# Plain float32 matmuls in the first chunk, with the split of its weights moved: one fused attention and MoE kernel

## The chip, the cores and the metric

The kernel runs on one core of a Trainium2 chip. The core has five engines that work side by side from their own queues: TensorE (PE, matmuls; PEld its weight loads), VectorE (DVE), ScalarE (ACT), GpSimd (POOL) and SyncE (SP), which here issues most DMAs. The metric is the device time of one execution in microseconds (us); lower is better.

## The reference, cut to what matters

Three layers follow each other on 4 x 576 = 2304 tokens. First windowed attention with 8 heads of 64; then a dense layer; then a layer with 8 experts, of which each token takes one.

```python
scores = scale * q @ k.T, kept where 0 <= row - col < 64
x = softmax(scores) @ v                       # 2304 x 512
h = x @ w_in                                  # w_in 512 x 2048
g = where(h >= 1, h, where(h <= -1, 0, (h + 1) ** 2 / 4))
x = g @ w_out                                 # w_out 2048 x 512
logits = x @ w_gate + modality_bias[modality_id]
e = argmax(logits);  out = gate_w * relu(x @ w1[e]) @ w2[e]
```

`w_in` and `w_out` come as 64 bit floats. [...]

## The kernel before

**Chunks and steps.** The tokens are cut into 6 chunks of 384 (`CT`). One chunk goes through 16 steps (`NF`), one for each block of 128 hidden units. Step f has `l1(c, f)`: 4 blocks of `w_in` against the chunk's x, result h in PSUM (2 buffers); then `act2` and `gsplit`; and, two steps later (`LAG`), `l2(c, f)`: matmuls of 512 columns that add to three sums `py`. Between the steps the attention of the next chunk's six blocks of 64 tokens is computed (`att_sc`, `att_exp`, `att_norm`, `att_tr`, `att_pv`, `att_x`); chunk 0's own six blocks run ahead of everything. After the chunk, `route` finds the experts. From some 520 us on, the expert layer runs in slots of 256 tokens; the change leaves it alone but for the names of the weight tiles.

**Precision by parts.** TensorE reads each operand as a rounded type, float32r. A float32 operand is kept as a rounded part (`hi`: a ScalarE copy) and the rest (`lo`: a subtraction), and a product is three matmuls: hi hi, hi lo, lo hi. So `l1` is 12 matmuls of 384 columns (L370) and `l2` 9 of 512 (L396). The scores (L292), the transposes (L330) and attention's second product (L345) are matmuls in plain float32.

**Decoding.** Chunk 0 is where the weights are decoded. They come in 16 pairs of 128 x 512 tiles: pair p, from 3 on, is block p - 1 of `w_out` and block p + 1 of `w_in`. The pair's words are loaded by SyncE (L237) to one of two buffers in `dec`. ScalarE takes the absolute value (`dec_abs`, L243). VectorE then runs four instructions for each tile: `dec_clamp` (L250, L252) and `dec_merge` (L258, L262). `dec_split` rounds on ScalarE (L270) and subtracts on GpSimd (L272), into `bigA` for `w_in` and `wB` for `w_out`. GpSimd also has `gsplit`'s subtraction in chunk 0 (L386) and `att_norm`'s multiplication (L323). Three pairs are decoded ahead of chunk 0 (`PRE`); then one in each step.

**Order.** A scheduler sets the order in the engines' queues from its own timeline; each queue then runs in that order. Only SyncE's order is written out by hand.

Of the kernel before, what the change touches and what calls it, by code (L numbers as in the profile page):

```python
# [9 lines left out]
F32 = mybir.dt.float32  # L10
F32R = mybir.dt.float32r
# [6 lines left out]
P = 128  # L18
# [52 lines left out]
def moe_kernel(ctx, tc, qT, kT, v, w_in, w_out, mod, wg, wgT, mbias, w1, w2, cst, tri, empty, out, spec):  # L71
# [11 lines left out]
        shape[axis] = n  # L83
        return a.broadcast_to(shape)

    WIDE = {"bigA", "dec", "prod", "q", "k", "v", "xh", "xl", "y", "s", "ts", "u", "gh", "gl"}
    WIDE |= {f"B{f}" for f in range(NF)}

    def tile_of(shape, name, dt=F32, tag=None, bufs=1):
        pool = sb if (tag or name) in WIDE else sm  # L90
# [3 lines left out]
        return ps.tile(shape, F32, name=name, tag="aux", bufs=3)  # L94

    WB = KD * P
    bigA = tile_of([P, NF * 2 * WB], "bigA", F32R)
    bigB, lent = {}, {}

    def piece(b, n):  # L100
        if not b:
            return bigA[:, n * WB : (n + 1) * WB]
        f, lo = divmod(n, 2)
        if f not in bigB:
            bigB[f] = tile_of([P, 2 * WB], f"wB{f}", F32R, tag=f"B{f}")
        return bigB[f][:, lo * WB : (lo + 1) * WB]

    def lend(f, lo, n=WB):
        if f not in lent:
            lent[f] = tile_of([P, 2 * WB], f"lent{f}", tag=f"B{f}")  # L110
        return lent[f][:, lo * WB : lo * WB + n]

    GB = 2
# [3 lines left out]

    def load_q(i):
        if i < BPC - 2:
            t = lend(2 + i // 2, i % 2)  # L120
        else:
            t = tile_of([P, WB], f"q{i}", tag="q", bufs=2)
        SP.dma_start(t, qT[i])
        qs[i] = t.rearrange("p (k n) -> p k n", k=KD)

    def load_k(g):
        t0 = g * GT
        k0 = max(t0 - BLK, 0)
        if g * GB < BPC:
            k_t = lend(7 + g, 0, KD * (GT + BLK)).rearrange("p (k n) -> p k n", k=KD)  # L130
# [147 lines left out]
    def new_x(c):  # L278
        xs[c] = tuple(tile_of([P, KD, CT], f"x{s}{c}", F32R, tag=f"x{s}", bufs=2) for s in "hl")

    at, xos = {}, {}

    def att_sc(i):
        q_t = qs.pop(i)
        k_t, k0 = ks[i // GB]
        n, w0 = window(i)
        if i < BPC:
            sc = ps.tile([P, KD, P], F32, name=f"sc{i}", tag=f"y{i % TT}", bufs=1)
        else:
# [454 lines left out]
    def half_slot(i, g, x, mid):  # L744
# [50 lines left out]
    for n in range(BPC + 3):  # L795
# [30 lines left out]
    for n in range(len(its) + LAG):  # L826
# [155 lines left out]
```

## Time and profile before

| What | us |
|---|---|
| median of 3 runs (785.8 to 785.94) | 785.9 |
| the profiled execution | 785.36 |
| its span in the trace | 783.7 |
| TensorE busy in the span | 732.9 |
| VectorE, ScalarE, GpSimd busy | 519.8, 418.3, 215.8 |
| chunk 0, first L370 to last L396 on TensorE | 33.2 to 152.0 |
| chunk 1 behind it, to its last L396 | 152.0 to 231.9 |

How to read it: an engine's busy time is a sum over stages that have different limits, so the table by itself does not tell what a change of one stage is worth. The trace is read by stretches instead. A matmul's time in a row overlaps its neighbour's; what it costs in a stream is the distance from one start to the next, which the chain of work shows as the sum for several. The granted clock is a share of TensorE's full 2.4 GHz.

### The profile page before, as it was taken

Reading aid. Unit: us, or ns where it says so; the run is one execution under the profiler, and the core shown is the slowest. Engines: PE = TensorE matmul, PEld = TensorE weight load, DVE = VectorE, ACT = ScalarE, POOL = GpSimd, SP = SyncE. Lnnn points to the kernel's source line nnn. Section 1 sums busy time; section 2 is a strip of 40 time slices with the busy share of each in tenths; the row PEclk is TensorE's granted clock in tenths of the full one; section 3 lists DMA queues with packets and bytes.
Section 4 is the critical chain, followed back from the end, with each engine's and each line's share of the span. In section 5 each row is a group of like instructions: output and inputs, shape, how many; then the busy total and the mean of one; then the engine's idle time right before and its main releaser. Section 6 shows DMA issues by size and latency. Waiting matters only on the chain.

```text
span 783.7 us, 13640 instructions
## 1 busy us (share of the span) xinstructions
PE 732.9 (94%) x4547; PEld 650.7 (83%) x4547; DVE 519.8 (66%) x1449; ACT 418.3 (53%) x973; POOL 215.8 (28%) x266
## 2 busy tenths in 40 slices
PE   7389796999999999999999999989997999999995
PEld 6377575988898889888898889878886989998994
DVE  4999999596349643964396648845765575656560
ACT  5565666645454544555455445534425565555551
POOL 2665667311201120102010232031047144432100
PEclk9689898999999999999999999999998999999998
DMA  9564463521222231222122105235547776766650
GB/s 325 170 217 144 166 217 109 213 70 42 55 59 80 65 62 48 82 69 61 48 82 62 14 1 182 74 55 165 172 95 222 236 229 218 225 220 226 216 189 18
DMA packets 55776, 101.90 MB, mean 130 GB/s; under 512 B 8032, under 2 KB 17376, under 8 KB 55568
## 3 DMA queue, kind: packets, MB, share of 16 engines
q1 hardware_dynamic: 50976, 90.91, 37.6%
q0 software_dynamic: 4576, 9.79, 4.1%
q8 instruction: 38, 0.62, 0.4%
q14 instruction: 42, 0.34, 0.1%
q10 hardware_dynamic: 144, 0.24, 0.1%
HBM read 91.46 MB, written 9.83 MB: 129 GB/s over the span
## 4 chain that ended last, share of the span: by engine, by line
PE 75%; DVE 13%; DMA 6%; issue 4%; ACT 1%; POOL 0%; SPq 0%; POOLq 0%; ACTq 0%; DVEq 0%
PE h L370 22%; PE py L396 22%; PE hp L707 11%; PE yo L730 11%; DMA wr<-in_w 3%; DVE dt L258 3%; PE sc L292 3%; DVE dt L250 3%; DVE dt L262 2%; PE xo L345 2%; DVE dt L252 1%; PE pt L330 1%; PE tp L693 1%; DMA dec<-in_w_in 1%; DVE u L379 1%
## 5 line engine op out<-in xcount | busy, mean ns | idle before, releaser
L370 PE MATMUL h<-xh,bigA 128*128 128x384 f32 x768 | 225.3, 354 | 15.4 <-DVE u L379 13.5
L396 PE MATMUL py<-wB,gh 128*128 128x512 f32 x576 | 181.8, 399 | 0.0
L370 PEld LDWEIGHTS h<-xh,bigA 128*128 128x128 f32 x768 | 144.0, 194 | 21.0 <-DVE u L379 15.5
L370 PE MATMUL h<-xl,bigA 128*128 128x384 f32 x384 | 132.1, 344 | 3.1 <-DVE xl L360 3.1
L396 PEld LDWEIGHTS py<-wB,gh 128*128 128x128 f32 x576 | 108.2, 192 | 17.2
L396 PE MATMUL py<-wB,gl 128*128 128x512 f32 x288 | 113.2, 398 | 0.9 <-POOL gl L386 0.8
L379 DVE SCALAR_TENSOR_TENSOR u<-u,h 128x384 f32<-128x384 f32 x96 | 52.9, 551 | 79.8 <-ACT u L374 78.4
L323 POOL TENSOR_TENSOR s<-s,sm 128x512 f32<-128x512 f32 (+1 forms) x30 | 34.2, 1140 | 220.6 <-DVE sm L322 95.7
L373 ACT ACTIVATE u<-h,half 128x384 f32<-128x384 f32 x96 | 55.3, 576 | 69.5 <-PE h L370 68.7
L453 DVE CUSTOM_DVE_ANT_0 prod<-y,wgb 128x512 f32<-128x512 f32 x120 | 85.4, 712 | 1.2
L385 ACT CAST gh<-u 128x384 fp32r<-128x384 f32 x96 | 49.3, 513 | 64.3 <-PE py L396 33.8
L370 PEld LDWEIGHTS h<-xl,bigA 128*128 128x128 f32 x384 | 74.7, 195 | 5.3 <-DVE xl L360 3.6
L643 ACT CAST bigA<-wr 128x512 fp32r<-128x512 f32 x80 | 48.5, 619 | 46.1 <-DMA wr<-in_w 40.2
L644 DVE TENSOR_TENSOR bigA<-wr,bigA 128x512 fp32r<-128x512 f32 x80 | 53.7, 688 | 27.7 <-ACT bigA L643 22.3
L644 DVE TENSOR_TENSOR wB<-wr,wB 128x512 fp32r<-128x512 f32 x80 | 53.1, 686 | 25.9 <-ACT wB L643 24.5
L396 PEld LDWEIGHTS py<-wB,gl 128*128 128x128 f32 x288 | 54.3, 189 | 14.4 <-POOL gl L386 3.0
L386 DVE TENSOR_TENSOR gl<-u,gh 128x384 fp32r<-128x384 f32 x80 | 45.0, 563 | 30.6 <-ACT gh L385 29.2
L643 ACT CAST wB<-wr 128x512 fp32r<-128x512 f32 x80 | 47.7, 619 | 27.2 <-DMA wr<-in_w 26.9
L738 POOL DMA_INDIRECT out<-ob,oi x19 | 20.0, 1051 | 153.0 <-ACT ob L737 119.0
L707 PE MATMUL hp<-zh,bigA 128*128 128x256 f32 x320 | 61.5, 288 | 0.0
L312 ACT ACTIVATE s<-s,mx 128x128 f32<-128x128 f32 (+1 forms) x120 | 46.1, 386 | 28.1 <-DVE mx L302 28.1
L730 PE MATMUL yo<-bigA,hm 128*128 128x512 f32 x240 | 57.5, 392 | 0.0
(203 smaller groups left out, 1324.9 us busy)
## 6 DMA issues: line engine op xcount, KB each, us to landing
wr<-in_w SPq DMA_DIRECT2D x160, 256.0 KB, 3.7
q<-in_qT SPq DMA_DIRECT2D x32, 256.0 KB, 3.8
dec<-in_w_in SPq DMA_DIRECT2D x16, 512.0 KB, 5.3
dec<-in_w_out SPq DMA_DIRECT2D x16, 512.0 KB, 3.7
v<-in_v SPq DMA_DIRECT2D x27, 256.0 KB, 2.5
k<-in_kT SPq DMA_DIRECT2D x15, 384.0 KB, 4.3
yd<-y SPq DMA_DIRECT2D x18, 256.0 KB, 2.8
wgb<-in_wgT SPq DMA_DIRECT2D x1, 2048.0 KB
```

The costliest lines, as they stand in the source:

```text
L312: A.activation(s[:, hp, :n], s[:, hp, :n], AF.Exp, bias=mx[:, hp : hp + 1], scale=-1.0, accum_out=sm[:, hp : hp + 1],)
L370: T.matmul(h, wi(f, a)[:, k, :], b[:, k, :], start=n == 0, stop=n == 3 * KD - 1)
L373: A.activation(u, h, AF.Relu, bias=half, scale=0.5)
L379: V.scalar_tensor_tensor(u, u, 1.0, h, op0=ALU.min, op1=ALU.max)
L385: A.copy(gh, u)
L386: (V if c else G).tensor_tensor(gl, u, gh.bitcast(F32), op=ALU.subtract)
L396: T.matmul(ys[c][t], a[:, sl], wo(f, b), start=f == 0 and n == 0, stop=f == NF - 1 and n == 2)
L453: V.tensor_tensor_reduce(prod, yt[t], wgb[0][:, e, :], 1.0, 0.0, ALU.mult, ALU.add, lg[:, t, e : e + 1])
L643: A.copy(wpart(i, p, 0), t)
L644: V.tensor_tensor(wpart(i, p, 1), t, wpart(i, p, 0).bitcast(F32), op=ALU.subtract)
L707: T.matmul(hp[:, u, :], w1s(i, 2 * fp + u, k, a), b[:, k, :], start=n == 0, stop=n == 3 * KD - 1,)
L730: T.matmul(yo, a[:, f, sl], w2s(i, f, b), start=n == 0, stop=n == 3 * NF2 - 1)
```

## The change

In chunk 0 the products are plain float32: `l1` is 4 matmuls of 384 columns and `l2` 3 of 512, on the decoded weights whole (`whole`), on an x that is not split, and on a g that is not split. The last decoding instruction writes the whole weight to a tile `raw` rather than in place. The two rounded parts are made by a new function `split`, ScalarE's copy and VectorE's subtraction; the code calls it for 6 weights in each of the last three steps of chunk 0 and for 2 in each step of chunk 1. `bigA` and the `wB` tiles become 32 tiles with the tags T0 to T31, which hold whole words first and parts later. GpSimd has none of the split; its normalisation of chunk 0's attention blocks goes to VectorE, that of chunk 1's blocks to ScalarE as four copies with a scale.

```diff
-    bigA = tile_of([P, NF * 2 * WB], "bigA", F32R)
+    def raw_home(p, u):
+        j = 2 * p + u
+        if j == 2 * NF - 1:
+            return dts[p][u]
+        if j // 2 not in raws:
+            raws[j // 2] = tile_of([P, 2 * WB], f"raw{j // 2}", I32, tag=f"T{j // 2}")
+        return raws[j // 2][:, j % 2 * WB : (j % 2 + 1) * WB]
...
             for u in range(2):
+                w = raw_home(p, u)
                 V.scalar_tensor_tensor(
-                    t[u], words(p, u)[0], 29, t[u], op0=ALU.logical_shift_right, op1=ALU.bitwise_or
+                    w, words(p, u)[0], 29, t[u], op0=ALU.logical_shift_right, op1=ALU.bitwise_or
                 )
-
-    def dec_split(p):
-        if p < NPR:
-            t = dts.pop(p)
-            for u, (kind, f) in enumerate(pairs[p]):
-                A.copy(piece(kind, 2 * f), t[u].bitcast(F32))
-            for u, (kind, f) in enumerate(pairs[p]):
-                G.tensor_tensor(
-                    piece(kind, 2 * f + 1), t[u].bitcast(F32), piece(kind, 2 * f).bitcast(F32), op=ALU.subtract
-                )
+                whole[pairs[p][u]] = w.bitcast(F32)
+    whole = {}
+    splits = [kf for p in pairs for kf in p]
+
+    def split(n):
+        for kind, f in splits[:n]:
+            k = len(parts)
+            tag = f"T{2 * NF - 2 + k if k < 2 else NF - 2 + k if k < NF else k - NF}"
+            t = tile_of([P, 2 * WB], f"w{kind}_{f}", F32R, tag=tag)
+            parts[kind, f] = (t, tag)
+            w = whole.pop((kind, f))
+            hi, lo = t[:, :WB], t[:, WB:]
+            A.copy(hi, w)
+            V.tensor_tensor(lo, w, hi.bitcast(F32), op=ALU.subtract)
+        del splits[:n]
...
-        G.tensor_tensor(s, s, bc(sm, 2, window(i)[0]), op=ALU.mult)
+        if BPC <= i < 2 * BPC:
+            w = window(i)[0]
+            for hp in range(KD):
+                A.activation(s[:, hp, :w], s[:, hp, :w], AF.Copy, scale=sm[:, hp : hp + 1])
+            return
+        (V if i < BPC else G).tensor_tensor(s, s, bc(sm, 2, window(i)[0]), op=ALU.mult)
...
-        for k in range(KD):
+        for k in range(KD if c == 0 else 0):
+            T.matmul(h, whole[0, f][:, k * P : (k + 1) * P], xs[c][:, k, :], start=k == 0, stop=k == KD - 1)
+        xh, xl = xs[c] if c else (None, None)
+        for k in range(KD if c else 0):
...
+        if c == 0:
+            g = gs.pop((c, f))
+            for t in range(TT):
+                T.matmul(
+                    ys[c][t], g[:, t * P : (t + 1) * P], whole[1, f], start=f == 0, stop=f == NF - 1
+                )
+            return
...
-            dec_split(f + PRE - 1)
             dec_abs(f + PRE)
+        if c == 0 and f >= NF - PRE:
+            split(6)
+        if c == 1:
+            split(2)
```

The order that results is told here at three places. On GpSimd, early in chunk 0, before (`bigA` and `wB` are weight parts, `gl` is the rest of g):

```order
35 L272 TENSOR_TENSOR bigA<-dt_0_391,bigA 128x512
36 L272 TENSOR_TENSOR wB_440<-dt_1_392,wB_440 128x512
37 L272 TENSOR_TENSOR wB_506<-dt_0_444,wB_506 128x512
38 L272 TENSOR_TENSOR bigA<-dt_1_445,bigA 128x512
39 L386 TENSOR_TENSOR gl_0_500<-u_0_485,gh_0_499 128x384
40 L272 TENSOR_TENSOR wB_568<-dt_0_511,wB_568 128x512
```

and now; the last two rows are for blocks 12 and 13, which are chunk 2's attention:

```order
22 L179 TENSOR_TENSOR btok<-modf,mb 128x144
23 L180 TENSOR_TENSOR btmp<-modn,mb 128x144
24 L181 TENSOR_TENSOR btok<-btok,btmp 128x144
25 L346 TENSOR_TENSOR s_1158<-s_1158,sm_1168 128x512
26 L346 TENSOR_TENSOR s_1249<-s_1249,sm_1261 128x512
```

GpSimd's queue holds nothing between the token biases and chunk 2's attention. On VectorE, around step 3 of chunk 0, before (`dt` are weights being decoded, `u` is the activation):

```order
137 L250 TENSOR_SCALAR dt_0_635<-dt_0_635 128x512
138 L258 SCALAR_TENSOR_TENSOR dt_1_574<-dec,dt_1_574 128x512
139 L252 TENSOR_SCALAR dt_0_635<-dt_0_635 128x512
140 L250 TENSOR_SCALAR dt_1_636<-dt_1_636 128x512
141 L262 SCALAR_TENSOR_TENSOR dt_1_574<-dec,dt_1_574 128x512
142 L379 SCALAR_TENSOR_TENSOR u_3_652<-u_3_652,h_3_639 128x384
143 L258 SCALAR_TENSOR_TENSOR dt_0_635<-dec,dt_0_635 128x512
```

and now (L258, L260, L266, L271 are the four decoding lines, L288 the split, L410 the activation):

```order
142 L410 SCALAR_TENSOR_TENSOR g_3_597<-u_3_580,h_3_575 128x384
143 L266 SCALAR_TENSOR_TENSOR dt_0_527<-dec,dt_0_527 128x512
144 L260 TENSOR_SCALAR dt_1_528<-dt_1_528 128x512
145 L288 TENSOR_TENSOR w_3_1082<-raw_498,w_3_1082 128x512
146 L288 TENSOR_TENSOR w_5_1085<-raw_498,w_5_1085 128x512
147 L271 SCALAR_TENSOR_TENSOR raw_545<-dec,dt_0_527 128x512
148 L266 SCALAR_TENSOR_TENSOR dt_1_528<-dec,dt_1_528 128x512
149 L258 TENSOR_SCALAR dt_0_571<-dt_0_571 128x512
150 L410 SCALAR_TENSOR_TENSOR g_4_656<-u_4_639,h_4_634 128x384
```

The scheduler has drawn the splits forward: they stand behind the decoding of their weights all through chunk 0, and the last of the 32 stands ahead of chunk 0's routing. On TensorE, at the end of chunk 0, before (`py` are the sums; `h_0_1433` and `h_1_1466` are chunk 1's steps 0 and 1):

```order
293 L370 MATMUL h_0_1433<-xh_450,bigA 128x384
294 L396 MATMUL py_0_603<-wB_1295,gh_14_1366 128x512 x2
295 L396 MATMUL py_0_603<-wB_1295,gl_14_1367 128x512
296 L396 MATMUL py_1_604<-wB_1295,gh_14_1366 128x512 x2
297 L396 MATMUL py_1_604<-wB_1295,gl_14_1367 128x512
298 L396 MATMUL py_2_605<-wB_1295,gh_14_1366 128x512 x2
299 L396 MATMUL py_2_605<-wB_1295,gl_14_1367 128x512
300 L370 MATMUL h_1_1466<-xh_450,bigA 128x384
```

and now:

```order
118 L428 MATMUL py_0_550<-raw_1019,g_14_1107 128x512
119 L428 MATMUL py_1_551<-raw_1019,g_14_1107 128x512
120 L428 MATMUL py_2_552<-raw_1019,g_14_1107 128x512
121 L428 MATMUL py_0_550<-dt_1_1002,g_15_1151 128x512
122 L428 MATMUL py_1_551<-dt_1_1002,g_15_1151 128x512
123 L428 MATMUL py_2_552<-dt_1_1002,g_15_1151 128x512
124 L310 MATMUL sc_1244<-k_953,q_955 128x128 x2
125 L398 MATMUL h_0_1179<-xh_431,w_0_1038 128x384
126 L398 MATMUL h_1_1212<-xh_431,w_1_1041 128x384
```

Chunk 0's last `l2` now stand in a row and all of chunk 1's `l1` behind them; before, two of chunk 1's `l1` ran ahead of them. From chunk 2 on the queues hold what they held, but for two or three weight loads' places at the end of chunk 5.

## Rows read from the trace of the kernel before

**Rows 1.** Busy time in stretches of 20 us: us, then busy us (and instructions) of PE, PEld, DVE, ACT and POOL, TensorE's granted clock, DMA share, GB/s.

```profile
20.00:40.00 20.00, 8.27 (x66) 6.79 (x67) 19.96 (x33) 11.21 (x27) 12.95 (x12) 0.60 0.58 176
40.00:60.00 20.00, 16.37 (x81) 14.53 (x81) 19.90 (x44) 14.10 (x38) 12.09 (x10) 0.89 0.63 207
...
120.00:140.00 20.00, 14.83 (x87) 12.61 (x86) 18.31 (x26) 11.42 (x28) 14.83 (x11) 0.83 0.40 125
```

**Rows 2.** The same columns for chunk 0 from its first L370, for chunk 1 and for chunk 2.

```profile
33.20:152.00 118.80, 97.29 (x538) 84.10 (x539) 109.08 (x209) 72.96 (x177) 72.12 (x53) 0.90 0.55 185
152.00:231.90 79.90, 79.90 (x511) 71.18 (x510) 48.84 (x185) 41.77 (x112) 9.80 (x10) 1.00 0.23 63
231.90:311.90 80.00, 80.00 (x511) 71.24 (x510) 48.65 (x185) 41.96 (x112) 10.07 (x10) 1.00 0.27 65
```

**Rows 3.** The longest waits of one engine for another between 33.2 and 152 us: who waited for whom, us in total, times, longest; here TensorE's for the activation.

```profile
PE h L370 <- DVE u L379: 11.5, 6, 4.2
```

**Rows 4.** Groups of instructions by line and shape, 0 to 160 us: line, engine, operation, names, shapes, count | busy us, mean ns | idle before, releaser.

```profile
L258 DVE SCALAR_TENSOR_TENSOR dt<-dec,dt 128x512 int32<-128x512 int32 x32 | 33.4, 1052 | 0.1
...
L252 DVE TENSOR_SCALAR dt<-dt 128x512 int32<-128x512 int32 x32 | 26.3, 828 | 0.1
L262 DVE SCALAR_TENSOR_TENSOR dt<-dec,dt 128x512 int32<-128x512 int32 x32 | 25.5, 799 | 0.0
L250 DVE TENSOR_SCALAR dt<-dt 128x512 f32<-128x512 f32 x32 | 24.9, 779 | 0.0
L272 POOL TENSOR_TENSOR bigA<-dt,bigA 128x512 fp32r<-128x512 f32 x16 | 24.6, 1535 | 13.0 <-ACT bigA L270 13.0
L272 POOL TENSOR_TENSOR wB<-dt,wB 128x512 fp32r<-128x512 f32 x16 | 24.0, 1504 | 16.4 <-ACT wB L270 14.4 <-DMA dec<-in_w_in 2.0
...
L386 POOL TENSOR_TENSOR gl<-u,gh 128x384 fp32r<-128x384 f32 x16 | 20.5, 1282 | 9.8 <-issue 6.1 <-ACT gh L385 3.7
```

**Rows 5.** Single instructions in order of time, VectorE's and GpSimd's: start us, us, engine, line, operation.

```profile
18.24 0.42 DVE L250 TENSOR_SCALAR dt<-dt 128x512 f32<-128x512 f32 x1
...
20.94 0.43 DVE L250 TENSOR_SCALAR dt<-dt 128x512 f32<-128x512 f32 x1
21.28 0.42 DVE L360 TENSOR_TENSOR xl<-xo,xh 128x256 fp32r<-128x256 f32 x1
...
22.58 0.69 DVE L258 SCALAR_TENSOR_TENSOR dt<-dec,dt 128x512 int32<-128x512 int32 x1
23.19 0.16 DVE L321 TENSOR_SCALAR sm<-sm 128x4 f32<-128x4 f32 x1
...
23.60 0.68 DVE L262 SCALAR_TENSOR_TENSOR dt<-dec,dt 128x512 int32<-128x512 int32 x1
...
23.85 1.55 POOL L272 TENSOR_TENSOR bigA<-dt,bigA 128x512 fp32r<-128x512 f32 x1 [1.59 <-ACT bigA L270]
...
24.29 2.58 DVE L250 TENSOR_SCALAR dt<-dt 128x512 f32<-128x512 f32 x2
...
35.90 0.41 DVE L252 TENSOR_SCALAR dt<-dt 128x512 int32<-128x512 int32 x1
36.23 0.68 DVE L262 SCALAR_TENSOR_TENSOR dt<-dec,dt 128x512 int32<-128x512 int32 x1
```

**Rows 6.** The chain of work that ended last, from 128 to 160 us: start us, us, what, and in how many records.

```profile
130.61 4.21 PE h L370 x12
...
138.61 0.61 PE xo L345 x16
...
147.82 2.10 PE h L370 x12
149.92 2.08 PE py L396 x9
152.00 0.89 PE sc L292 x8
...
157.30 0.22 PE pt L330 x2
```

**Rows 7.** The same view from 0 to 180 us, two pieces of VectorE's.

```profile
47.81 0.20 DVE s L302
...
130.09 0.47 DVE u L379
```

**Rows 8.** One group of the expert layer, from the page: VectorE's subtraction for a 128x512 weight part; columns as in rows 4.

```profile
L644 DVE TENSOR_TENSOR wB<-wr,wB 128x512 fp32r<-128x512 f32 x80 | 53.1, 686 | 25.9 <-ACT wB L643 24.5
```

**Rows 9.** Single instructions around chunk 0's start: SyncE's issues, ScalarE's absolute values and x copies, TensorE's first matmul.

```profile
24.34 7.04 SPq L237 DMA_DIRECT2D dec<-in_w_out  x2
...
32.78 0.37 ACT L359 CAST xh<-xo 128x256 fp32r<-128x256 f32 x1
...
33.20 1.01 PE L370 MATMUL h<-xh,bigA 128*128 128x384 f32 x2 [1.59 <-ACT xh L359]
...
34.59 0.67 ACT L243 ACTIVATE dt<-dec 128x512 f32<-128x512 f32 x1 [1.44 <-DMA dec<-in_w_out]
```

**Rows 10.** DMA issues of the words up to 140 us: what, engine, count, KB each, median us from issue to landing.

```profile
dec<-in_w_in SPq DMA_DIRECT2D x16, 512.0 KB, 5.3
dec<-in_w_out SPq DMA_DIRECT2D x16, 512.0 KB, 3.7
```

More of the change, by code (lines that the diff above doesn't have):

```diff
@@ L84, in bc @@
         return a.broadcast_to(shape)
-    WIDE = {"bigA", "dec", "prod", "q", "k", "v", "xh", "xl", "y", "s", "ts", "u", "gh", "gl"}
-    WIDE |= {f"B{f}" for f in range(NF)}
+    WIDE = {"dec", "prod", "q", "k", "v", "xh", "xl", "y", "s", "ts", "u", "gh", "gl"}
+    WIDE |= {f"T{f}" for f in range(2 * NF)}
     def tile_of(shape, name, dt=F32, tag=None, bufs=1):
@@ L96, in moe_kernel @@
     WB = KD * P
-    bigA = tile_of([P, NF * 2 * WB], "bigA", F32R)
-    bigB, lent = {}, {}
+    raws, parts, experts, lent = {}, {}, {}, {}
     def piece(b, n):
-        if not b:
-            return bigA[:, n * WB : (n + 1) * WB]
         f, lo = divmod(n, 2)
-        if f not in bigB:
-            bigB[f] = tile_of([P, 2 * WB], f"wB{f}", F32R, tag=f"B{f}")
-        return bigB[f][:, lo * WB : (lo + 1) * WB]
+        if (b, f) not in experts:
+            experts[b, f] = tile_of([P, 2 * WB], f"e{b}_{f}", F32R, tag=parts[b, f][1])
+        return experts[b, f][:, lo * WB : (lo + 1) * WB]
     def lend(f, lo, n=WB):
         if f not in lent:
-            lent[f] = tile_of([P, 2 * WB], f"lent{f}", tag=f"B{f}")
+            lent[f] = tile_of([P, 2 * WB], f"lent{f}", tag=f"T{NF + f}")
         return lent[f][:, lo * WB : lo * WB + n]
@@ L119, in load_q @@
         if i < BPC - 2:
-            t = lend(2 + i // 2, i % 2)
+            t = lend(i // 2, i % 2)
         else:
@@ L129, in load_k @@
         if g * GB < BPC:
-            k_t = lend(7 + g, 0, KD * (GT + BLK)).rearrange("p (k n) -> p k n", k=KD)
+            k_t = lend(5 + g, 0, KD * (GT + BLK)).rearrange("p (k n) -> p k n", k=KD)
         else:
@@ L146, in load_v @@
             return
-        vs[i] = lend(4 + i // 2, i % 2) if i < BPC else tile_of([P, DM], f"v{i}", tag="v", bufs=2)
+        vs[i] = lend(2 + i // 2, i % 2) if i < BPC else tile_of([P, DM], f"v{i}", tag="v", bufs=2)
         SP.dma_start(vs[i][:n], v[w0 : w0 + n, :])
@@ L207, in moe_kernel, with part @@
     PRE = 3
+    def part(kind, f, lo):
+        return parts[kind, f][0][:, lo * WB : (lo + 1) * WB]
+    def raw_home(p, u):
[5 more added lines that the diff above has]
+        return raws[j // 2][:, j % 2 * WB : (j % 2 + 1) * WB]
     def wi(f, lo):
-        return piece(0, 2 * f + lo).rearrange("p (k n) -> p k n", k=KD)
+        return part(0, f, lo).rearrange("p (k n) -> p k n", k=KD)
     def wo(f, lo):
-        return piece(1, 2 * f + lo)
+        return part(1, f, lo)
     c0 = float(np.array([896 << 20], np.uint32).view(np.float32)[0])
@@ L261, in dec_merge @@
             for u in range(2):
+                w = raw_home(p, u)
                 V.scalar_tensor_tensor(
-                    t[u], words(p, u)[0], 29, t[u], op0=ALU.logical_shift_right, op1=ALU.bitwise_or
+                    w, words(p, u)[0], 29, t[u], op0=ALU.logical_shift_right, op1=ALU.bitwise_or
                 )
-    def dec_split(p):
-        if p < NPR:
-            t = dts.pop(p)
-            for u, (kind, f) in enumerate(pairs[p]):
-                A.copy(piece(kind, 2 * f), t[u].bitcast(F32))
-            for u, (kind, f) in enumerate(pairs[p]):
-                G.tensor_tensor(
-                    piece(kind, 2 * f + 1), t[u].bitcast(F32), piece(kind, 2 * f).bitcast(F32), op=ALU.subtract
-                )
+                whole[pairs[p][u]] = w.bitcast(F32)
[12 more added lines that the diff above has]
+        del splits[:n]
     xs = {}
     def new_x(c):
+        if c == 0:
+            xs[c] = tile_of([P, KD, CT], "x0", tag="xh", bufs=2)
+            return
         xs[c] = tuple(tile_of([P, KD, CT], f"x{s}{c}", F32R, tag=f"x{s}", bufs=2) for s in "hl")
@@ L295, in att_sc @@
         if i < BPC:
-            s = lend(10 + i, 0).rearrange("p (k n) -> p k n", k=KD)
+            s = lend(8 + i, 0).rearrange("p (k n) -> p k n", k=KD)
         else:
@@ L331, in att_tr @@
         if i < BPC:
-            ts = lend(10 + i, 1).rearrange("p (k n) -> p k n", k=KD)
+            ts = lend(8 + i, 1).rearrange("p (k n) -> p k n", k=KD)
         else:
@@ L356, in att_x @@
         c, n = divmod(i, BPC)
+        dst = slice(n * BLK, (n + 1) * BLK)
+        if c == 0:
+            A.copy(xs[c][:, :, dst], xo)
+            return
         xh, xl = xs[c]
-        dst = slice(n * BLK, (n + 1) * BLK)
         A.copy(xh[:, :, dst], xo)
@@ L364, in l1 @@
     def l1(c, f):
-        xh, xl = xs[c]
         h = ps.tile([P, CT], F32, tag="h", name=f"h{c}_{f}", bufs=2)
         n = 0
-        for k in range(KD):
+        for k in range(KD if c == 0 else 0):
+            T.matmul(h, whole[0, f][:, k * P : (k + 1) * P], xs[c][:, k, :], start=k == 0, stop=k == KD - 1)
+        xh, xl = xs[c] if c else (None, None)
+        for k in range(KD if c else 0):
             for a, b in ((0, xh), (0, xl), (1, xh)):
@@ L378, in act2 @@
         u, h = us[c, f], hs.pop((c, f))
-        V.scalar_tensor_tensor(u, u, 1.0, h, op0=ALU.min, op1=ALU.max)
+        g = u
+        if c == 0:
+            g = gs[c, f] = tile_of([P, CT], f"g{c}_{f}", tag="gh" if f % 2 else "gl", bufs=2)
+        V.scalar_tensor_tensor(g, u, 1.0, h, op0=ALU.min, op1=ALU.max)
     def gsplit(c, f):
         u = us.pop((c, f))
+        if c == 0:
+            return
         gh = tile_of([P, CT], f"gh{c}_{f}", F32R, tag="gh", bufs=2)
@@ L385, in gsplit @@
         A.copy(gh, u)
-        (V if c else G).tensor_tensor(gl, u, gh.bitcast(F32), op=ALU.subtract)
+        V.tensor_tensor(gl, u, gh.bitcast(F32), op=ALU.subtract)
         gs[c, f] = (gh, gl)
@@ L391, in l2 @@
             ys[c] = [ps.tile([P, DM], F32, tag=f"y{t}", name=f"py{c}_{t}", bufs=1) for t in range(TT)]
+        if c == 0:
+            g = gs.pop((c, f))
[3 more added lines that the diff above has]
+                )
+            return
         gh, gl = gs.pop((c, f))
@@ L750, in l1 @@
             hp = ps.tile([P, 2, P], F32, tag="h", name=f"hp{i}_{fp}", bufs=2)
-            w = [bigB[lo * NP // 2 + fp].rearrange("p (q k n) -> p k q n", q=2, k=KD) for lo in range(2)]
+            w = [experts[1, lo * NP // 2 + fp].rearrange("p (q k n) -> p k q n", q=2, k=KD) for lo in range(2)]
             n = 0
@@ L811, in moe_kernel @@
             if m % 2:
-                dec_split(m // 2)
                 dec_abs(m // 2 + 1)
```

## The prediction, made before the changed kernel ran

> **What bounds the kernel now.** I read the stretches first. From 152 us on TensorE is busy all the time, at full clock, and chunks 1 and 2 take 79.9 and 80.0 us [rows 2]; nothing that frees another engine moves these. Chunk 0 takes 118.8 us for the same count of matmuls, with TensorE busy 97.3 us of it at a mean clock of 0.90 [rows 2]. In the stretches from 20 to 60 us, and at 120, VectorE is busy 18.3 to 20.0 of each 20 us, while TensorE has gaps and its clock falls to 0.60 and 0.83 [rows 1]. TensorE's longest wait there is for VectorE's activation u, 11.5 us [rows 3]: VectorE comes to it late. So chunk 0 is set by VectorE.
>
> Why VectorE is slow is to be seen in single instructions. L250 starts at 20.94 and the next instruction at 21.28, L252 at 35.90 and the next at 36.23, L258 at 22.58 and the next at 23.19: in a stream these cost 0.34, 0.33 and 0.61 us, and L262, which lasts as long as L258, the same 0.61 less a hundredth [rows 5]. But as GpSimd's L272 begins at 23.85 and lasts 1.55, two L250 take 2.58 us [rows 5]. Over chunk 0 the four lines' means are 779 to 1052 ns and their sum 24.9 + 26.3 + 33.4 + 25.5 = 110.1 us [rows 4]. GpSimd's subtractions stretch VectorE's decoding.
>
> **The change, part by part.**
>
> Decoding. With GpSimd's queue empty, 32 weights cost 32 x (0.34 + 0.33 + 0.61 + 0.60) = 60.2 us in place of 110.1. Bounds: 60.2, and 110.1 if the stretching has another cause.
>
> What VectorE gets. 32 splits at 0.686 us, 0.61 in a stream if they follow each other as L258 does [rows 5, 8]: 19.5 us. The order shows them inside chunk 0, not behind it, so all count there. From VectorE's first decoding instruction, at 18.2 us [rows 5], to its last split the queue holds: decoding 60.2, splits 19.5, 16 activations at 0.47 = 7.5, 7 blocks of scores at 4 x 0.20 = 5.6 [rows 7], 18 small ones at 0.16 = 2.9, 6 subtractions of x at 0.34 = 2.0 and two normalisations at 0.61 = 1.2 [rows 5]. That is 98.9 us; without a wait it ends at 117.1.
>
> TensorE's matmuls. The trace of before has no plain float32 matmul of 384 or 512 columns. The nearest are the scores: 4 matmuls of 128 columns are 8 records in 0.89 us, 0.111 each [rows 6]. A rounded matmul of 384 columns costs 2.10 / 12 = 0.175 and one of 512 columns 2.08 / 9 = 0.231 [rows 6], so 0.056 for 128 columns: each record of the scores streams its columns twice, each matmul four times. By columns, a float32 matmul of 384 is 2 x 3 x 0.111 = 0.67 us and one of 512 is 2 x 4 x 0.111 = 0.89. A step is then 4 x 0.67 + 3 x 0.89 = 5.34 us instead of 2.10 + 2.08 = 4.18: dearer by 1.16, or 18.6 us over 16 steps, although it has 7 matmuls for 21. The low end takes the fixed 0.007 us of a rounded matmul (0.175 - 3 x 0.056) out of the part that scales: 5.09 a step. The high end prices each stream as a rounded matmul: 4 x 4 x 0.175 + 3 x 4 x 0.231 = 5.57. I take 5.34, from the same kind of matmul.
>
> Here the Trainium skill speaks against the change. Its page FP8 and Floating Point Precision, section TensorE Precision Notes, says that true FP32 takes four passes through the array, against the three of the split product that it replaces; the scores' row agrees on four. By the page alone, at the rounded passes' price, a step would be 5.57 and the kernel's time 3.7 us above my sum.
>
> Chunk 0's start. `h_0` needs the last copy of x, and in ScalarE's new order this stands behind the absolute value of weight (1, 1), whose words are loaded when pair 0's second weight is merged. By VectorE's queue that is at 18.2 + 6 = 24.2, as before (24.34 [rows 9]); the next load of this kind was issued at the end of the 7.04 us, 31.05, and used at 34.59, 3.5 us later [rows 9]. So 24.3 + 3.5 + 0.67 + 0.37 gives 29 us. Before, the first L370 was at 33.20 [rows 9], and VectorE's x parts held the rest back. With x whole, nothing more is waited for.
>
> The sum for chunk 0: start 29.0; TensorE comes to it cold, and a cold `l1` costs 4.21 in place of 2.10 [rows 6], so 2.1 lost; 16 steps at 5.34 = 85.4; attention 7 x 0.89 + 6 x 2 x 0.22 + 6 x 0.61 = 12.5 [rows 6]. End at 129.0. For waits between queues that run in fixed orders I add 2: 131. VectorE stays ahead: step 15's weight is merged at 108 us by its sum, and TensorE wants it at 116; the activations, which free the two buffers of h, are 4 to 8 us ahead of the `l1` that reuse them. Words: 512 KB take 3.7 to 5.3 us to land [rows 10], and each buffer has 5 to 6 us between its merge and the next clamp, so a few of these loads will be felt; the lead and the 2 us cover that. The price of the lead gone is the rival below.
>
> ScalarE loses 16 roundings of g and gets 24 scalings of 128 x 128; it was busy 73.0 of 118.8 us [rows 2], and hides both. GpSimd's idleness costs nothing. The 32 tiles: a part's tile is free once earlier weights were split and multiplied; the last ones wait for steps 13 and 14, and stand behind all decoding, so only VectorE's routing is behind them.
>
> Chunk 1. Two of its `l1` stood before chunk 0's end and now stand behind it: 79.9 + 2 x 2.10 = 84.1 us. VectorE's 48.8 of 79.9 us [rows 2] do not grow, as the splits are done. It ends at 131 + 84.1 = 215.1 instead of 231.9: 16.8 us sooner. Behind that both queues hold the same work, TensorE full. Execution 785.36 - 16.8 = 768.6 us. The profiled execution is 0.5 us below the median of 785.9, which I leave aside.
>
> **The rivals.**
>
> VectorE keeps the pace. If loads, ScalarE's copies and fixed orders make a pair take 7.5 us, where its share of the queue is 6, then from pair 2's merge at 33 us pair 14 comes at 33 + 12 x 7.5 = 123; behind it `l1` of step 15, three `l2` and attention, 4 x 2.67 + 1.5 = 12.2, end chunk 0 at 135, and the kernel at 773; at 8 us a pair, 779. Against: by the sum TensorE needs no pair sooner than each 5.9 us, and the point from which it decides is 7.1.
>
> TensorE stays cold (the slower end). Four streams make clock time dearer: 97.9 us of matmuls at full clock. Before, the gaps brought a mean of 0.90 [rows 2]. If VectorE leaves gaps as now and the mean falls to 0.80, chunk 0 is 29 + 97.9 / 0.80 + 2 = 153, chunk 1 ends at 237, the kernel at 791. It turns into a loss when chunk 0 ends past 231.9 - 84.1 = 147.8, a mean clock below 0.84. Against: the wanted TensorE time per step rises to 5.9 us with attention, the wait for VectorE shrinks, so there should be few gaps.
>
> The change doesn't free VectorE: the stretching comes from ScalarE or the DMAs, not GpSimd. Then VectorE's queue is 148.8 us and ends at 167; chunk 0 ends near 165 and the kernel near 803. Against: the pair of 0.34 and 2.58 / 2 within 4 us, with the loads going on in both [rows 5].
>
> **How the numbers follow.** Forecast 0.77; VectorE's pace 0.12; cold 0.05; not freed 0.03; 0.03 for the parts cancelling. Forecast's own range: 5.09 a step and no wait gives 768.6 - 4.0 - 2 = 762.6; 5.57 and 4 us more of waits 768.6 + 3.7 + 4 = 776.3. The pace rival fills the range up to 779, and leaves out the other three cases and a little below. A measurement of this kernel tells 0.2%, 1.6 us, from no change: faster 0.77 + 0.12 + 0.01, within 0.02, slower 0.05 + 0.03.
>
> **What would show it.** Right: L258 to L271 (the new decoding lines) with means of 0.42 to 0.7 us; the first plain `l1` near 29 us; 8 records of 384 columns in 2.7 us and 6 of 512 in 2.7; chunk 0's last `l2` near 131 with a clock over 0.95 from 35 us on; chunk 1 in 84 us. Wrong: decoding means of 0.8 us or more; records far from 0.33 and 0.44; TensorE waiting for `raw` or g in most steps; a clock under 0.9; or a gain that chunk 1 or the expert layer gives back.

## The result, and the profile after

The changed kernel takes 765.97 us, median of 4 runs (765.01 to 766.82); the kernel before, in the same measurement, 785.92 (785.8 to 786.64). The ratio is 0.9744, interval 0.9727 to 0.9761. In a second measurement the two took 765.22 and 781.62 us, ratio 0.9795 [0.9759, 0.9831]. Forecast was 768.6 us, by the ratio 0.978.

The busy time of the changed kernel in stretches (columns as in [rows 1]), the last three of them chunks 0, 1 and 2:

```profile
20.00:40.00 20.00, 14.78 (x91) 9.99 (x92) 18.78 (x39) 14.16 (x31) 3.06 (x5) 0.74 0.65 205
40.00:60.00 20.00, 20.00 (x59) 10.47 (x58) 19.57 (x56) 15.63 (x44) 0.00 (x0) 1.00 0.67 230
...
120.00:140.00 20.00, 20.00 (x115) 14.43 (x113) 14.69 (x52) 11.36 (x32) 1.60 (x2) 1.00 0.52 188
29.19:129.83 100.64, 99.57 (x402) 55.34 (x403) 90.05 (x238) 71.53 (x181) 1.04 (x1) 0.98 0.66 220
129.83:214.36 84.53, 84.53 (x534) 75.55 (x534) 49.17 (x186) 44.39 (x117) 9.58 (x10) 1.00 0.24 60
214.36:294.30 79.94, 79.94 (x510) 71.19 (x510) 48.66 (x185) 41.96 (x112) 10.39 (x10) 1.00 0.27 65
```

Beside [rows 1, 2]: chunk 0 shrinks from 118.8 to 100.6 us and TensorE is busy 99.57 of them, so it, and no longer VectorE, bounds the chunk. The granted clock is 1.00, the level of 2.4 GHz, from 40 us on; it was 0.74 in the stretch before, in which TensorE starts its row of matmuls at 29.19. Chunk 1 is longer by the two `l1` that it took over, 84.5 us, and chunk 2 is what it was. Chunk 1 ends at 214.36 instead of 231.9.

VectorE's groups in the first 140 us (columns as in [rows 4]) and the end of its decoding, in time:

```profile
L266 DVE SCALAR_TENSOR_TENSOR dt<-dec,dt 128x512 int32<-128x512 int32 x32 | 21.9, 686 | 0.0
L271 DVE SCALAR_TENSOR_TENSOR raw<-dec,dt 128x512 int32<-128x512 int32 x31 | 21.5, 693 | 0.0
L288 DVE TENSOR_TENSOR w<-raw,w 128x512 fp32r<-128x512 f32 x31 | 21.4, 694 | 2.3 <-ACT w L287 2.3
L260 DVE TENSOR_SCALAR dt<-dt 128x512 int32<-128x512 int32 x32 | 13.5, 431 | 0.0
L258 DVE TENSOR_SCALAR dt<-dt 128x512 f32<-128x512 f32 x32 | 13.5, 423 | 3.0 <-ACT dt L251 3.0
```

```profile
116.58 0.69 DVE L271 SCALAR_TENSOR_TENSOR dt<-dec,dt 128x512 int32<-128x512 int32 x1
```

The four decoding lines fall from 110.1 [rows 4] to 21.9 + 21.5 + 13.5 + 13.5 = 70.4 us busy, each at about the duration it had where GpSimd did not run beside it [rows 5], and the last weight is whole at 117.3 us.

TensorE's first matmuls of chunk 0, TensorE in the chain of work (as in [rows 6]), late in chunk 0, and what ScalarE waits for between 28 and 135 us (as in [rows 3]):

```profile
29.19 7.42 PE L394 MATMUL h<-x,raw 128*128 128x384 f32 x16 [2.27 <-ACT x L382]
```

```profile
103.68 2.58 PE py L428 x6
106.26 2.58 PE h L394 x8
```

```profile
ACT dt L251 <- DMA dec<-in_w_out: 10.8, 10, 2.3
ACT dt L251 <- DMA dec<-in_w_in: 7.9, 9, 1.8
```

A float32 matmul shows as two records, so the two rows of the chain are the 3 matmuls of an `l2` and the 4 of an `l1`. A step is 2.58 + 2.58 = 5.16 us. ScalarE still waits in most steps for the words to land (each 64 bit weight is read as two words of 32 bits), 18.7 us in all. TensorE does not show these waits: it was idle for 100.64 - 99.57 = 1.1 us of the chunk.

### The profile page after: what moved, and what is told of

The parts are those of the page before. It is cut to its first block, busy times and chain, and to the rows that moved or that the text cites. A ratio compares the mean times of both kernels' runs of the same rounds, so it can differ in the third digit from the quotient of the medians.

```text
span 763.6 us, 13319 instructions
## 1 busy us (share of the span) xinstructions
PE 736.9 (97%) x4435; PEld 623.2 (82%) x4435; DVE 499.2 (65%) x1481; ACT 419.7 (55%) x981; POOL 132.8 (17%) x206
## 4 chain that ended last, share of the span: by engine, by line
PE 76%; DMA 10%; DVE 7%; ACT 4%; issue 2%; POOL 0%; POOLq 0%; SPq 0%; ACTq 0%; DVEq 0%
PE h L398 22%; PE py L436 21%; PE hp L747 10%; PE yo L770 9%; DMA wr<-in_w 5%; PE sc L310 4%; DMA dec<-in_w_in 3%; PE xo L368 2%; PE py L428 2%; PE pt L353 2%; DVE raw L271 1%; DVE e L684 1%; PE h L394 1%; DVE dt L266 1%; PE tp L733 1%
## 5 line engine op out<-in xcount | busy, mean ns | idle before, releaser
L398 PE MATMUL h<-xh,w 128*128 128x384 f32 x640 | 182.7, 345 | 0.2 <-DVE u L410 0.2
L436 PE MATMUL py<-w,gh 128*128 128x512 f32 x480 | 149.4, 393 | 0.0
L684 DVE TENSOR_TENSOR e<-wr,e 128x512 fp32r<-128x512 f32 x160 | 106.9, 688 | 52.4 <-ACT e L683 49.9
L683 ACT CAST e<-wr 128x512 fp32r<-128x512 f32 x160 | 96.1, 619 | 69.2 <-DMA wr<-in_w 63.5
L398 PEld LDWEIGHTS h<-xh,w 128*128 128x128 f32 x640 | 116.3, 188 | 3.2 <-DVE u L410 0.6
L770 PE MATMUL yo<-e,hm 128*128 128x512 f32 x456 | 110.2, 392 | 0.9 <-ACT hm L755 0.8
L747 PE MATMUL hp<-zh,e 128*128 128x256 f32 x576 | 110.1, 286 | 0.1
L398 PE MATMUL h<-xl,w 128*128 128x384 f32 x320 | 107.5, 336 | 0.0
L410 DVE SCALAR_TENSOR_TENSOR u<-u,h 128x384 f32<-128x384 f32 x80 | 44.3, 554 | 77.7 <-ACT u L402 77.5
L436 PE MATMUL py<-w,gl 128*128 128x512 f32 x240 | 94.1, 396 | 0.0
L747 PEld LDWEIGHTS hp<-zh,e 128*128 128x128 f32 x576 | 92.4, 193 | 0.8 <-ACT zh L735 0.3
L330 ACT ACTIVATE s<-s,mx 128x128 f32<-128x128 f32 (+1 forms) x120 | 46.1, 386 | 22.5 <-DVE mx L320 22.5
```

The source lines that it names most:

```text
L330: A.activation(s[:, hp, :n], s[:, hp, :n], AF.Exp, bias=mx[:, hp : hp + 1], scale=-1.0, accum_out=sm[:, hp : hp + 1],)
L410: V.scalar_tensor_tensor(g, u, 1.0, h, op0=ALU.min, op1=ALU.max)
L436: T.matmul(ys[c][t], a[:, sl], wo(f, b), start=f == 0 and n == 0, stop=f == NF - 1 and n == 2)
L683: A.copy(wpart(i, p, 0), t)
L684: V.tensor_tensor(wpart(i, p, 1), t, wpart(i, p, 0).bitcast(F32), op=ALU.subtract)
L747: T.matmul(hp[:, u, :], w1s(i, 2 * fp + u, k, a), b[:, k, :], start=n == 0, stop=n == 3 * KD - 1,)
```

## The experiments

Each kernel's chunk ends are read as the end of its last `l2`. The first four ran on one chip, where the kernel before took 783.85 us (median of 15 runs, 781.28 to 787.53); the last three on another.

### The split goes back to GpSimd

```diff
-            V.tensor_tensor(lo, w, hi.bitcast(F32), op=ALU.subtract)
+            G.tensor_tensor(lo, w, hi.bitcast(F32), op=ALU.subtract)
```

> The changed kernel with one word changed: the split's subtraction runs on GpSimd again, the plain float32 matmuls stay. Theory (GpSimd's work beside VectorE stretches the decoding): before, 72 us of GpSimd work in chunk 0 went with 50 us of stretching; 32 subtractions at 1.52 us are 49 us, so some 34 us of stretching against 19.5 us taken off VectorE. Its queue ends 14 us later, half of that is covered by its lead over TensorE: 773 us, decoding means 0.55 to 0.9 us. Rival (the gain comes from fewer instructions on the path, not from GpSimd's silence): VectorE is relieved of 19.5 us, 766 us or less, decoding means as in the changed kernel (0.42 to 0.69 us).

Measured: 778.35 us, ratio 0.9934 [0.9908, 0.9961]. Chunk 1 ends at 228.94, 14.6 us later than in the changed kernel. Groups of the first 160 us, TensorE's wait between 30 and 150 us, and a few single instructions in order of time:

```profile
L271 DVE SCALAR_TENSOR_TENSOR raw<-dec,dt 128x512 int32<-128x512 int32 x31 | 27.3, 887 | 0.1
L266 DVE SCALAR_TENSOR_TENSOR dt<-dec,dt 128x512 int32<-128x512 int32 x32 | 25.8, 813 | 0.1
L260 DVE TENSOR_SCALAR dt<-dt 128x512 int32<-128x512 int32 x32 | 19.9, 628 | 0.1
L258 DVE TENSOR_SCALAR dt<-dt 128x512 f32<-128x512 f32 x32 | 19.2, 606 | 0.4 <-ACT dt L251 0.4
...
L288 POOL TENSOR_TENSOR w<-raw,w 128x512 fp32r<-128x512 f32 x31 | 46.3, 1496 | 86.3 <-ACT w L287 82.8 <-DVE g L410 3.2 <-DVE dt L258 0.3
```

```profile
PE h L394 <- DVE g L410: 6.8, 4, 2.1
```

```profile
58.88 1.27 POOL L288 TENSOR_TENSOR w<-raw,w 128x512 fp32r<-128x512 f32 x1 [2.01 <-ACT w L287]
58.98 1.72 DVE L266 SCALAR_TENSOR_TENSOR dt<-dec,dt 128x512 int32<-128x512 int32 x1
60.62 0.42 DVE L258 TENSOR_SCALAR dt<-dt 128x512 f32<-128x512 f32 x1
60.96 0.68 DVE L271 SCALAR_TENSOR_TENSOR raw<-dec,dt 128x512 int32<-128x512 int32 x1
```

With 32 subtractions fewer on VectorE the decoding there is 92.2 us, 21.8 more than in the changed kernel: as much as the 32 subtractions cost it (21.4 for 31 of them). L266 takes 1.72 us where it starts just behind a GpSimd subtraction, and L271 0.68 two instructions later. So work given to GpSimd here is paid on VectorE all the same. The rival, decoding means as in the changed kernel, is out; the theory was right in kind but had 34 us of stretching and 773 us.

Why it costs 14.6 us is less plain: the last weight is whole at 116.2 us, as early as before the edit. What differs is that TensorE waits for g, 6.8 us in 4 waits of up to 2.1, and its clock falls to between 0.91 and 0.98 in the three stretches from 60 to 120 us. The scheduler also laid the queues anew for this kernel, with the decoding further ahead: from step 4 on the weight of an `l1` is whole 9 to 22 us before that `l1` starts, in the changed kernel 4.5 to 7.7 us, and g comes late behind it. So a part of the 14.6 us may be the order's; this run does not part them.

### GpSimd made busy beside the changed kernel

```diff
+                G.tensor_tensor(junk, w.bitcast(F32), w.bitcast(F32), op=ALU.subtract)
...
+    junk = tile_of([P, WB], "junk", tag="xl", bufs=2)
```

Everything of the change stays; GpSimd subtracts each finished weight from itself into a tile that nothing reads.

> The changed kernel with 32 added GpSimd subtractions of 128 x 512, one behind each decoded weight, into a tile that nobody reads; nothing waits for them. Theory: they stretch VectorE's decoding by some 30 us, more than its lead of 8, so chunk 0 ends some 20 us later: 780 to 790 us. Rival (the stretching comes from ScalarE or the DMAs): no change, 766 us.

Measured: 781.18 us, ratio 0.9976 [0.9956, 0.9996]: the gain is all but gone. VectorE's five groups in the first 160 us, single instructions in order of time, the last decoding, and TensorE's longest wait between 28 and 150 us:

```profile
L266 DVE SCALAR_TENSOR_TENSOR dt<-dec,dt 128x512 int32<-128x512 int32 x32 | 25.4, 796 | 0.0
L290 DVE TENSOR_TENSOR w<-raw,w 128x512 fp32r<-128x512 f32 x31 | 23.4, 759 | 1.9 <-ACT w L289 1.9
L260 DVE TENSOR_SCALAR dt<-dt 128x512 int32<-128x512 int32 x32 | 22.5, 709 | 0.0
L271 DVE SCALAR_TENSOR_TENSOR raw<-dec,dt 128x512 int32<-128x512 int32 x31 | 21.9, 705 | 0.0
L258 DVE TENSOR_SCALAR dt<-dt 128x512 f32<-128x512 f32 x32 | 18.5, 583 | 0.0
```

```profile
59.81 0.68 DVE L266 SCALAR_TENSOR_TENSOR dt<-dec,dt 128x512 int32<-128x512 int32 x1
60.04 1.35 POOL L275 TENSOR_TENSOR junk<-raw 128x512 f32<-128x512 f32 x1 [2.23 <-DVE raw L271]
60.41 1.26 DVE L258 TENSOR_SCALAR dt<-dt 128x512 f32<-128x512 f32 x1
...
62.06 0.42 DVE L258 TENSOR_SCALAR dt<-dt 128x512 f32<-128x512 f32 x1
...
63.22 1.09 POOL L275 TENSOR_TENSOR junk<-raw 128x512 f32<-128x512 f32 x1 [1.83 <-DVE raw L271]
63.33 1.52 DVE L290 TENSOR_TENSOR w<-raw,w 128x512 fp32r<-128x512 f32 x1
64.78 0.41 DVE L260 TENSOR_SCALAR dt<-dt 128x512 int32<-128x512 int32 x1
```

```profile
134.47 0.68 DVE L271 SCALAR_TENSOR_TENSOR dt<-dec,dt 128x512 int32<-128x512 int32 x1
```

```profile
PE pt L355 <- ACT s L346: 7.9, 2, 4.4
```

L258 is 1.26 us when it meets GpSimd's subtraction and 0.42 when it does not; the split's subtraction (L290 here) 1.52 and 0.68. The five groups sum to 25.4 + 23.4 + 22.5 + 21.9 + 18.5 = 111.7 us against 91.8: 19.9 us for 32 GpSimd instructions, 0.62 each. That is less than the 30 us of the theory; the time is in its range. The last weight is whole at 135.2 instead of 117.3, 17.9 us later, and chunk 1 ends at 231.78, 17.4 us later. Nothing waits for `junk`, and apart from the 32 added subtractions every engine runs the same instructions in the same order as in the changed kernel; this is the shown cause. It does not reach TensorE by the weights of `l1`, which from step 4 on are whole 1.6 us or more before their use, but by the other work in VectorE's queue: the longest waits, 7.9 of 10.5 us of idle time in chunk 0, are for the next chunk's scores, which ScalarE can normalise only behind VectorE's reciprocal. TensorE's mean clock in the chunk falls from 0.98 to 0.93.

### GpSimd idle, all matmuls rounded

The kernel before, with its GpSimd work of chunk 0 moved away as the change moves it, and its three rounded matmuls for each product kept:

```diff
@@ dec_split
-                G.tensor_tensor(
+                V.tensor_tensor(
@@ att_norm
-        G.tensor_tensor(s, s, bc(sm, 2, window(i)[0]), op=ALU.mult)
+        if BPC <= i < 2 * BPC:
+            w = window(i)[0]
+            for hp in range(KD):
+                A.activation(s[:, hp, :w], s[:, hp, :w], AF.Copy, scale=sm[:, hp : hp + 1])
+            return
+        (V if i < BPC else G).tensor_tensor(s, s, bc(sm, 2, window(i)[0]), op=ALU.mult)
@@ gsplit
-        (V if c else G).tensor_tensor(gl, u, gh.bitcast(F32), op=ALU.subtract)
+        V.tensor_tensor(gl, u, gh.bitcast(F32), op=ALU.subtract)
```

> The kernel before with only GpSimd's share of chunk 0 moved: both subtractions of rounded parts and the normalisation of chunk 0's blocks on VectorE, that of chunk 1's blocks on ScalarE; every matmul of both layers stays a rounded product of three. Theory (GpSimd's silence is the whole gain, and plain float32 costs TensorE about 1 us a step): VectorE's queue is 60.2 + 19.5 + 7.7 for g's rest and 21 more, 108.5 us, ends near 127; TensorE's step is 4.18 and no longer the bound; chunk 0 ends near 125 and the kernel near 759 us, below the changed kernel. Rival (plain float32 is needed, since the rounding and the subtraction stand between a weight's decoding and its first product): 770 us or more.

Measured: 767.4 us, ratio 0.9783 [0.9744, 0.9821]; chunk 1 ends at 214.69. Stretches, VectorE's subtraction of g with its group, and the last decoding:

```profile
40.00:60.00 20.00, 18.29 (x108) 15.37 (x107) 19.85 (x58) 18.11 (x51) 0.00 (x0) 1.00 0.65 217
...
100.00:120.00 20.00, 15.61 (x86) 11.95 (x86) 19.28 (x44) 15.12 (x35) 0.00 (x0) 1.00 0.65 223
```

```profile
L391 DVE TENSOR_TENSOR gl<-u,gh 128x384 fp32r<-128x384 f32 x18 | 9.9, 552 | 0.6 <-ACT gh L390 0.6
```

```profile
127.24 0.69 DVE L262 SCALAR_TENSOR_TENSOR dt<-dec,dt 128x512 int32<-128x512 int32 x1
```

Without one plain float32 product the end of chunk 1 is within 0.4 us of the changed kernel's (214.36), and the ratios' intervals overlap. So taking GpSimd's work away brings alone what the change brings. The time under the changed kernel's that my theory wanted here did not come, nor the rival's 770 us: TensorE has less to do, but VectorE is busy 19.0 to 20.0 of each 20 us from 40 to 120 us. It carries the subtractions of g, 9.9 us, and its last weight is whole at 127.9, 10.7 us behind the changed kernel's. TensorE's waits are short, for ScalarE's rounded copies as well as for VectorE's parts. ScalarE waits 13.3 us for words to land here, so that VectorE alone bounds the chunk is likely but not shown.

### The early normalisations back on GpSimd

The changed kernel with `att_norm` as it was, all 12 early blocks on GpSimd:

```diff
-        if BPC <= i < 2 * BPC:
-            w = window(i)[0]
-            for hp in range(KD):
-                A.activation(s[:, hp, :w], s[:, hp, :w], AF.Copy, scale=sm[:, hp : hp + 1])
-            return
-        (V if i < BPC else G).tensor_tensor(s, s, bc(sm, 2, window(i)[0]), op=ALU.mult)
+        G.tensor_tensor(s, s, bc(sm, 2, window(i)[0]), op=ALU.mult)
```

> The changed kernel with the normalisation of the twelve early attention blocks on GpSimd as before. Theory: GpSimd works 13 us in all, 7 of them ahead of chunk 0's start, where block 5's normalisation is on the path to x, and each stretches one or two of VectorE's instructions; chunk 0 starts 1 to 2 us later and the rest is covered by VectorE's lead: 767 to 769 us. Rival (any GpSimd work in chunk 0 costs its full length): 775 us or more.

Measured: 765.21 us, ratio 0.9766 [0.973, 0.9802], no difference from the change that can be told, and a little under the 767 to 769 us of the theory. GpSimd's groups in the first 160 us:

```profile
L341 POOL TENSOR_TENSOR s<-s,sm 128x512 f32<-128x512 f32 x8 | 11.0, 1370 | 99.4 <-DVE sm L340 71.8 <-ACT w L287 22.0 <-PE pt L348 5.7
L341 POOL TENSOR_TENSOR lent<-lent,sm 128x512 f32<-128x512 f32 x5 | 5.4, 1070 | 8.2 <-DVE sm L340 6.5 <-ACT lent L330 1.2 <-ACT lent L353 0.4
```

The stretching is there (L260's mean is 501 ns for 431), but a dozen such instructions fit into what TensorE, still busy 98.73 of 100 us from 40 to 140 us, leaves VectorE. Chunk 1 ends at 215.54, 1.2 us later. This part of the change is worth nothing that could be measured.

### Layer one rounded, layer two plain

The changed kernel with the plain product kept only for `l2`: in chunk 0 `w_in`'s weights are split as they are decoded and `l1` is 12 rounded matmuls on a split x; `w_out`'s are split three steps later. The tags of the 32 tiles are dealt out to fit.

```diff
-            xs[c] = tile_of([P, KD, CT], "x0", tag="xh", bufs=2)
...
-        for k in range(KD if c == 0 else 0):
-            T.matmul(h, whole[0, f][:, k * P : (k + 1) * P], xs[c][:, k, :], start=k == 0, stop=k == KD - 1)
-        xh, xl = xs[c] if c else (None, None)
-        for k in range(KD if c else 0):
+        xh, xl = xs[c]
+        for k in range(KD):
...
+            split_in(f + PRE - 1)
             dec_abs(f + PRE)
-        if c == 0 and f >= NF - PRE:
-            split(6)
-        if c == 1:
-            split(2)
+        if 3 <= n < 3 + NF:
+            split(1, n - 3)
```

> A mixture: in chunk 0 layer one is rounded (12 matmuls of 384 columns, x and the w_in tiles split as before, the split on VectorE at once), layer two stays plain float32 on whole w_out tiles, whose split follows three steps later; GpSimd stays out. TensorE's step falls from 5.16, as measured, to 2.10 + 2.58 = 4.68; VectorE gets 6 subtractions of x, 2 us. Theory (with GpSimd silent, chunk 0 of the changed kernel is bound by TensorE, and of the kernel with rounded products throughout by VectorE's and ScalarE's decoding): chunk 0 ends some 6 us sooner, 758 to 762 us. Rival (the loop of load, absolute value and merge through two buffers of words is the bound near 5.5 us a pair, whatever the products): 765 us or more, TensorE waiting for w_in parts.

Measured: 764.67 us (760.82 to 765.92), ratio 0.9765 [0.9724, 0.9806], beside 0.9795 for the changed kernel on the same chip: the same. The 758 to 762 us of the theory did not come; the rival's 765 or more was just missed. Chunk 1 ends at 213.47, 0.9 us sooner. A stretch, two waits between 76 and 104 us, and pieces of the chain of work that ends them:

```profile
80.00:100.00 20.00, 17.27 (x83) 11.78 (x83) 18.15 (x54) 14.45 (x40) 0.00 (x0) 0.91 0.59 190
```

```profile
PEld h L395 <- ACT w L287: 3.0, 1, 3.0
PE h L395 <- DVE g L407: 2.7, 1, 2.7
```

```profile
78.34 4.81 DMA dec<-in_w_in
...
83.23 0.67 ACT dt L254
...
87.52 0.98 PE h L395 x2
```

A rounded `l1` saves 2.58 - 2.10 = 0.48 us a step, 7.7 in all, but needs the split ahead of it. The first `l1` starts at 31.08, in the changed kernel's two profiles at 29.19 and 30.48; the last weight is whole at 122.5 for 117.3; and TensorE stands idle for 4.9 us of its chunk 0, at a mean clock of 0.96. More than half of that is the one gap before 87.52, which both waits shown end. Its chain goes back to words that land at 83.15: ScalarE's absolute value waits for them, and the activation stands behind it in ScalarE's queue. So, by this chain, the rival's loop of words through two buffers takes a part of what the cheaper products give; how large a part was not tested.

### The two kernels again

No edit; both were run a second time to see how far single profiles may be compared.

> The changed kernel unchanged, beside the mixture on one chip: 766 us. It also shows whether chunk 5, which took 65.8 us in its first trace, takes that again.

> The kernel before unchanged, for a second trace: if chunk 5's 69.2 us in its first trace, 3.4 more than in the changed kernel, is the landing of weight words beside GpSimd's gather, it may come out near 65.7 here, as in the run with only GpSimd's share moved, which has the same tiles; if it belongs to the kernel before, it is 69 again.

The changed kernel: 765.22 us (762.34 to 766.83); the one run of the kernel before 779.5. Chunk 5 in the first and the second profile of before, from the end of chunk 4's last `l2` to that of its own:

```profile
470.80:540.02 69.22, 67.17 (x340) 60.27 (x339) 47.67 (x134) 33.05 (x64) 14.16 (x22) 0.98 0.38 107
```

```profile
469.20:534.87 65.67, 65.61 (x340) 58.77 (x339) 47.75 (x134) 32.96 (x64) 15.22 (x22) 1.00 0.40 113
```

In the changed kernel chunk 5 took 65.82 us. The first pair of profiles had shown 3.4 us more gain there than at the end of chunk 1; the second profile of before shows that this is its own variation and not the change's. By the second pair the gain is 230.33 - 214.31 = 16.0 us at the end of chunk 1 and 534.87 - 519.05 = 15.8 at the end of chunk 5.

## Why the prediction was right

The forecast put the gain at the end of chunk 1, 16.8 us. It was 17.5 us there in the first pair of profiles and 16.0 in the second.

- **Decoding freed by GpSimd's idleness: right, and shown.** The means are 423 to 693 ns where 420 to 700 were named. Making GpSimd busy again, with nothing else changed, moves the last weight by 17.9 us and chunk 1's end by 17.4. The rival that the stretching comes from ScalarE or the DMAs falls with it. The Trainium skill's page SBUF — State Buffer, section Who interferes with whom, names VectorE's and GpSimd's shared port pair as the one place where engines block each other, with issue order deciding who waits; the rows at 58.98, 60.41 and 63.33, of instructions that start behind GpSimd's and end after it, agree.
- **VectorE's queue: the sum right, the waits left out.** Forecast were 98.9 us from 18.2 to 117.1, if nothing waits. VectorE was busy 99.9 us, but it took 110.7 for them: the last decoding ended at 117.3, and three splits came later, the last from 128.0 to 128.9, each behind a wait for ScalarE's copy. They stand behind all decoding, as the order had shown, and TensorE did not need them yet. The lead over TensorE was smaller than forecast: step 15's weight was whole at 113.1 and used at 117.7, 4.5 us ahead in place of 8.
- **The step of TensorE: mis-sized by a little.** 5.16 us in place of 5.34, inside its bounds of 5.09 and 5.57: 8 records of 384 columns in 2.58 us, 6 of 512 in 2.58. That is 0.18 x 16 = 2.9 us less. The scores' row that I scaled from holds 0.111 us per 128 columns [rows 6], these records 0.3225 / 3 = 0.1075 and 0.43 / 4 = 0.1075; why the short one is dearer was not followed up. By the Trainium skill's FP8 and Floating Point Precision, section TensorE Precision Notes, with a rounded matmul's price for each of the four passes, it would have been 5.57; two records of 0.3225 us, each nearly twice a rounded matmul's 0.175, agree with four passes, but a pass is then 0.161 us, not 0.175.
- **Chunk 0's start: 29.0 forecast, 29.19 measured.** So close a hit is partly luck: the second profile has 30.48. The first 16 records, cold, took 7.42 us where 16 x 0.3225 = 5.16 would do: 2.3 lost, 2.1 forecast.
- **Its end: 131 forecast, 129.83 measured.** 29.19 + 82.6 + 2.3 + the forecast attention of 12.5 is 126.6, so 3.2 us are left where I had put 2 for waits. Of these TensorE was idle for 1.1; the other 2.2 are attention, for which 99.57 - 82.6 - 2.3 = 14.7 us remain. I had put TensorE's step 2.9 too high, the waits 0.9 too high and the attention 2.2 too low: errors that cancel in part. Chunk 1 took 84.5 us, 84.1 forecast.
- **The rivals.** VectorE did not set the pace, nor did TensorE stay cold: its clock was 1.00 in every stretch from 40 us on. But the margin is thin. With some 20 us more on VectorE the run with GpSimd made busy fell back nearly to the time before, and the run with GpSimd idle and rounded products, with 10 more, lost all that these would save.
- **What the forecast did not say:** the plain products bring nothing by themselves. They cost TensorE 16 x (5.16 - 4.18) = 15.7 us and take the subtractions of g, 16 x 0.55 = 8.8 us, off VectorE, and the waits for rounded parts off TensorE. Four kernels show it by chunk 1's end: 231.9 us with rounded products and GpSimd at work, 214.7 with rounded products and GpSimd idle, 214.4 with plain ones and GpSimd idle, 231.8 with plain ones and GpSimd made busy. The gain is the idleness of GpSimd.

The measured gain, 20.0 us in the first measurement and 16.4 in the second, differs mainly by the kernel before (785.92 and 781.62 us). Where that kernel's 4 us between the two measurements come from, beyond chunk 5, was not followed up. A third buffer for the words was not tried, so how much the landing of words still holds back is open.

## What to carry to other kernels

Before work is moved to an idle GpSimd, look at what VectorE runs beside it: a GpSimd subtraction of some 1.35 us (the median; 1.04 to 2.03) cost VectorE 0.62 us on average here, so 32 of them cost what they would have cost on VectorE itself. Judge a change of one stage by the end of that stage in several profiles as well as by the total, since single profiles of the same kernel differed by 3.6 us in a stage far behind it. Where two engines are both nearly full, a cheaper form of the work on one is worth only what the other leaves.

## What the runs showed of the hardware

At the granted clock of 1.00 a plain float32 matmul of 384 columns costs 0.645 us in a stream and one of 512 columns 0.86, 3.7 times a rounded matmul of that size, 0.175 and 0.231 [rows 6]. So plain float32 costs 5.16 / 4.18 = 1.23 times the three rounded products, not 4/3, and needs no parts.

An instruction of VectorE that is already running when GpSimd's begins is not stretched: in the run with GpSimd made busy L266 ran 0.68 us from 59.81 while GpSimd's began at 60.04 and took 1.35 us, where the shortest took 1.04. Over that run's L258, the six that were running when a GpSimd instruction began took 410 ns on average, the sixteen with none beside them 415, and the ten that began behind one 956. Nor is every instruction stretched: the activation, which reads h from PSUM, has a mean of 542 ns there and 552 in the changed kernel.
